# Two reorderings in a fused attention and Fourier-mixing kernel: the order of seven block products, and a transpose taken apart

## The chip, the core and the metric

The kernel runs on one core of a Trainium2 chip. The core has engines that each work through their own list of instructions in order and wait for one another through semaphores: PE (TensorE: matmuls and transposes; its weight loads are shown apart as PEld), DVE (VectorE), ACT (ScalarE), POOL (GpSimd) and SP (SyncE, which here only issues DMA transfers). The metric is the time of one execution on the device in microseconds (us), the median of several runs.

## The reference

Two stages, for 8 batches of 576 tokens, 8 heads of 64 channels (512 channels in all).

```
scores = q @ k.T / 8                            # per batch and head, 576 x 576
keep the 32 largest of each row (>= the 32nd), others -1e9
x = softmax(scores) @ v                         # heads put side by side: 576 x 512
u = x + real(fft(fft(x, axis=tokens), axis=channels))
un = (u - mean(u)) / sqrt(var(u) + 1e-6)        # over the channels
out = u + relu(un @ w_ch1) @ w_ch2              # w_ch1: 512 x 2048, w_ch2: 2048 x 512
```

## The kernel before, in words

**Attention.** The 32 pairs of heads (four to a batch; `PER_PAIR` = 9 work items to a pair, `PER_BATCH` = 36 to a batch, 288 in all) run through one main loop over steps `i` (L1589). An item is 128 rows of scores. In step `i` PE makes the scores of item `i + 3`, ACT evicts them (L396, L414, L425), DVE finds the 32nd largest value of item `i` and `i + 1` by alternating MAX8 and MATCH_REPLACE8 (L446, L448: seven long instructions to an item), and ACT and POOL mask and exponentiate items `i - 1` and `i - 2` (L469, L472, L480). From the second batch on the probabilities go by ACT copies and DMA (L493, L506, L509) to DRAM and come back transposed (L527); PE then multiplies them by v (`attend`, L585), and the result is turned to token rows (`to_tokens`, L626) and normalised by DVE (L630).

**q and k.** `prep` (L309) transposes the next pair's q or k on PE (L329) into a PSUM tile with the tag `tp`, which has two buffers, and ACT evicts it (L337, L339). For q it is called at every step with `i % 9 == 0` from the second batch on, with two blocks: four 128-token blocks (the main block) go to one `tp` buffer, and the tail block, made of `qtail`, to the next one. The partial scores `sp_t` (L392, evicted at L396) use the same two buffers.

**The mixing and the two-layer product.** When a batch's attention is done, the Fourier mixing (POOL folds at L685 to L762, PE at L809 to L864) and the normalisation follow, and the two matmuls of the MLP are cut into units that wait in a list, `queue`. A unit is one hidden tile (`hidden`, L1046) or a part of the second product (`back`, L1075; `fast`, L1155). The units carry a planned cost in us (1.75 for most, 2.13 or 1.71 for a hidden tile). After each entry of the step's list `fixed` the loop calls `some`, which puts out units as long as the planned room of the step lasts, and after an entry that stands in `preps` at least up to a limit of 1.1, which is one unit:

```
got += some(max(room * (n + 1) / len(fixed) - got, 1.1 if fn in preps else 0.0))
```

What a step puts out over its room is carried over (`carry`) and taken from the room of the next.

**Seven products.** For the first chunk of batches 1 to 7 (counted from 0) and the second chunk of batches 6 and 7, `fast` makes the second product of four 128-token by 4 blocks with seven block products instead of eight. There are nine such places. Each of p1 to p7 is put out in two halves (`part` 0 and 1), and each half is a unit. Two PSUM banks are held throughout, `cv` and `cw`: p2 writes the low half of `cv`, p5 the high half, p3 adds to the high half; p1 writes the low half of `cw`, p4 its high half (in the last batch a third bank, `cz`), p6 and p7 add to the low half. After its second half each product is read out of its bank by ACT (L1225), in the last batch by DVE (L1211). Left factors are made in place by `mix` (L1193, run at L1198 on POOL, in the last steps on DVE): "21" before p5, "11" and "12" after p1, "22" after p4. Combined parts of the second weight matrix lie in DRAM (`scr`, shown as `w_parts`) and are fetched by `bring` (L973, L976, issued on SP) over the part that was used last: T1 into `w2_12` at the begin (for p5), T4 into `second` after each half of p2 (for p4), T2 into `w2_12` after each half of p5 (for p6), T3 into `second` after each half of p4 (for p7), then the originals back.

Of the kernel before, what the change touches and what calls it, by code (L numbers as in the profile page):

```python
# [86 lines left out]
def kernel(  # L87
# [15 lines left out]
    NC = 5  # L103
    NF = NC - 1
# [4 lines left out]
    NPB = H // 2  # L109
# [199 lines left out]
    def prep(n, pair, blocks=((0, NF), (NF, NC))):  # L309

        if pair >= NPAIR:
            return 0.0
        src, got_of = nat[n, pair], qT_of if n == "q" else kT_of
        if pair not in got_of:
            got_of[pair] = attp.tile(
                [P, S if n == "q" else NF * P], F32, name=f"{n}T_{pair}", tag=f"{n}T",
                bufs=2 if n == "q" else 1
            )
        t_sb = got_of[pair]
        for c0, c1 in blocks:  # L320
            tp = ps_t.tile([P, 4, P], F32, name=f"tp{n}_{pair}_{c0}", tag="tp")
            for c in range(c0, c1):
                block, turn_by = src[:, c, :, :], ident
                if n == "q":
                    turn_by = turns[:, 2 if c == NF else c % 2, :]
                    if c == NF:
                        hp = pair % NPB
                        block = qtail[:, 2 * hp:2 * hp + 2, :]
                nc.tensor.transpose(  # L329
                    tp[:, c - c0, :], block.rearrange("p h d -> p (h d)"), turn_by  # L330
                )
            if c0 < NF:
                dst, got = t_sb[:, c0 * P:c1 * P], tp.rearrange("p a c -> p (a c)")[:, 0:(c1 - c0) * P]
            else:
                dst, got = t_sb[:, NF * P:], tp[:, 0, 0:TAIL]
            if n == "q":
                nc.scalar.mul(out=dst, in_=got, mul=scale)  # L337
            elif c0 < NF:
                nc.scalar.copy(out=dst, in_=got)  # L339
            else:  # L340
                for e in range(2):
                    r = slice(D * e, D * (e + 1))
                    nc.scalar.copy(out=kt_t[r, TAIL * e:TAIL * (e + 1)], in_=tp[r, 0, 0:TAIL])
        return 0.7
# [696 lines left out]
    def mlp_units(b):  # L1041
        x = x_of[b]
        last = b == B - 1
# [111 lines left out]
        def fast(ch):  # L1155
# [164 lines left out]
            def begin():  # L1320
# [6 lines left out]
                (0.0, lambda: mix("21", "21", "22", ALU.add), "back")  # L1327
            ] + [
                (1.75, lambda f=f, part=part: f(part), "back")
                for f in (p2, p5, p1, p4, p6, *((p7, p3) if last and ch else (p3, p7)))  # L1330
                for part in range(2)
            ]

# [1 line left out]
        for ch in range(2):  # L1335
            units += [
                (8 * CW[ch] / 1200.0, lambda ch=ch, it=it: hidden(ch, it), ("hidden", b, ch))
                for it in range(NIT)
            ]
            seven = b and ch == 0 or b >= B - 2  # L1340
            if seven:
                begin, products = fast(ch)
                if ch == 0:
                    begins.append(begin)
                else:
                    units.insert(1 - NIT, (0.0, begin, ("hidden", b, 1)))
                mix_first = products.pop(0)
                units.append(mix_first)
            for t in [t for t in CHUNKS[ch] if t == 4 or not seven]:
                units += [  # L1350
                    (1.75, lambda ch=ch, t=t, p=p: back(ch, t, p), "back")
                    for p in range(4 if t == 4 else 8)
                ]
            if seven:
                units += products
# [127 lines left out]
    for b in range(B):  # L1483
        end = PER_BATCH * (b + 1) - 1
        last = b == B - 1
# [54 lines left out]
    def chunk_at(i):  # L1540

        for tile in (i - 5, i - 4, i - 3, i - 2):
            r = tile % PER_PAIR
            if PER_BATCH <= tile < N and r in (4, 8):
                if i - tile == ((5 if r == 4 else 4) if by_dma(tile) else 2 if tile in (2 * PER_BATCH - 1, N - 1) else 3):
                    return tile // PER_PAIR, r // 8
        return None, None
# [41 lines left out]
    while i < N + 5 or plan or queue or sums:  # L1589
        now[0] = i  # L1590
        run(i, "begin")
        pair_of = i // PER_PAIR
# [10 lines left out]
        preps = []  # L1603

        q_step = i == 2 if pair_of == 0 else i % PER_PAIR == 0
        if i < N and q_step:
            preps.append(lambda: prep("q", pair_of + 1))
        if i < N and i % PER_PAIR == 5:
            preps.append(lambda: prep("k", pair_of + 1))
        last_scores = []  # L1610
# [75 lines left out]
        pair, ch = chunk_at(i)  # L1686
# [81 lines left out]
```

## Time and profile before

| what | value |
|---|---|
| median of 3 runs | 1776.76 us (1775.06 to 1779.67) |
| the profiled execution | 1780.27 us, span from its first to its last instruction 1778.5 us |
| PE busy | 1632.1 us, 92% |
| DVE busy | 1552.5 us, 87% |
| ACT busy | 1278.8 us, 72% |
| POOL busy | 906.6 us, 51% |
| DMA queue of SP | 243.80 MB, 52.5% of 16 engines' span |

The times of the trace are those of the one profiled execution. A row of the timeline reads: start in us, length in us, engine, line, operation, what it writes and reads, shapes, how many instructions the row joins, and in brackets how long the engine had been idle and what ended that. A product of `fast` shows as 16 matmuls of 128x256. Because matmuls are pipelined, the time from the start of one group to the start of the next says more than the length of a group. `q` after an engine's name (SPq) means its issuing side.

### The profile page before, as it was taken

What the parts mean: (1) busy time and instruction counts of PE and PEld (TensorE: products, weight loads), DVE (VectorE), ACT (ScalarE), POOL (GpSimd) and SP (SyncE); (2) the same over time, 40 slices, a digit from 0 to 9 for tenths busy, and PEclk for the clock granted to TensorE, in tenths of its full rate; (3) what the DMA queues carried; (4) which work ended last, traced back from release to release, by engine and by line L of the source; (5) the groups of instructions that cost most, each with busy time, mean ns of one, the idle gap of its engine ahead of it and who ended that gap; (6) DMA issues with size and microseconds to landing.
All of it is one profiled execution on the core that took longest, in us unless ns stands there. A gap on an engine that the chain in (4) does not pass through costs nothing.

```text
span 1778.5 us, 26295 instructions
## 1 busy us (share of the span) xinstructions
PE 1632.1 (92%) x7830; PEld 1040.9 (59%) x7830; DVE 1552.5 (87%) x3319; ACT 1278.8 (72%) x3136; POOL 906.6 (51%) x1268
## 2 busy tenths in 40 slices
PE   5666689999898989999999999999999999999998
PEld 3444455464455755566555755576566755577777
DVE  7999989999999999998999999999999999863121
ACT  6888759887787878876888778877978787653200
POOL 4768846655634565354544665356535564333000
PEclk7778799999999999999999999999999999999999
DMA  5333126651457855586557856595558655643151
GB/s 156 115 102 117 32 81 163 185 152 50 119 145 196 222 131 135 136 233 161 135 136 200 212 133 140 152 240 145 152 132 222 182 135 128 172 114 101 36 180 60
DMA packets 492926, 255.28 MB, mean 144 GB/s; under 512 B 364528, under 2 KB 483056, under 8 KB 492784
## 3 DMA queue, kind: packets, MB, share of 16 engines
q1 hardware_dynamic: 489008, 243.80, 52.5%
q0 software_dynamic: 2816, 9.44, 1.6%
q8 instruction: 63, 1.03, 0.2%
q14 instruction: 79, 0.65, 0.1%
q10 hardware_dynamic: 960, 0.36, 0.1%
HBM read 99.79 MB, written 84.74 MB: 104 GB/s over the span
## 4 chain that ended last, share of the span: by engine, by line
PE 48%; DVE 16%; ACT 16%; POOL 14%; issue 5%; DMA 2%; POOLq 0%; SPq 0%; DVEq 0%; ACTq 0%
PE hp L1055 18%; DVE m L446 7%; DVE wk L448 6%; PE o L585 6%; PE cw L1254 5%; POOL wk L472 5%; PE cv L1254 4%; PE sp L422 4%; ACT wk L469 3%; POOL fold L696 3%; PE cp L1120 2%; ACT wk L493 2%; PE cp L1082 2%; ACT S L425 2%; PE sp_t L392 1%
## 5 line engine op out<-in xcount | busy, mean ns | idle before, releaser
L472 POOL TENSOR_TENSOR wk<-S,wk 128x576 f32<-128x576 f32 x288 | 407.6, 1415 | 418.1 <-ACT wk L469 417.2
L446 DVE MAX8 m<-wk 128x8 f32<-128x576 f32 x864 | 617.4, 741 | 0.1
L1055 PE MATMUL hp<-unT,w 128*128 128x256 f32 (+1 forms) x2048 | 529.6, 409 | 6.8 <-ACT hT L1059 6.0
L1055 PEld LDWEIGHTS hp<-unT,w 128*128 128x128 f32 x2048 | 378.0, 191 | 112.0 <-ACT hT L1059 11.4
L448 DVE MATCH_REPLACE8 wk<-m,wk 128x576 f32<-128x576 f32 x576 | 424.8, 737 | 0.0
L469 ACT ACTIVATE wk<-S,nt 128x576 f32<-128x576 f32 x288 | 224.3, 779 | 96.8 <-POOL nt L455 96.3
L493 ACT COPY wk<-S 128x576 uint16<-128x576 uint16 x468 | 290.2, 673 | 0.0
L446 DVE MAX8 m<-S 128x8 f32<-128x576 f32 x288 | 214.5, 745 | 11.6 <-ACT S L396 11.6
L480 ACT ACTIVATE S<-wk,nt 128x576 f32<-128x576 f32 x234 | 185.1, 791 | 46.7 <-POOL wk L472 45.4
L448 DVE MATCH_REPLACE8 wk<-m,S 128x576 f32<-128x576 f32 x288 | 212.5, 738 | 0.0
L1082 PE MATMUL cp<-w,hT 128*128 128x512 f32 x448 | 206.0, 598 | 0.0
L1059 ACT ACTIVATE hT<-hp 128x320 f32<-128x320 f32 (+1 forms) x256 | 104.1, 411 | 140.7 <-PE hp L1055 139.7
L585 PE MATMUL o<-PT,v 128*64 128x256 f32 (+3 forms) x1440 | 196.1, 417 | 5.6 <-DVE wk L448 2.1
L422 PE MATMUL sp<-kT,qT 64*128 64x512 f32 (+1 forms) x528 | 160.1, 668 | 6.7 <-ACT S L414 3.6
L585 PEld LDWEIGHTS o<-PT,v 128*64 128x64 f32 x1440 | 113.2, 154 | 84.1 <-issue 24.8
L425 ACT COPY S<-sp 128x512 f32<-128x512 f32 (+1 forms) x264 | 141.7, 589 | 26.2 <-PE sp L422 25.2
L455 POOL TENSOR_TENSOR nt<-m,cc 128x2 f32<-128x2 f32 x288 | 58.7, 204 | 166.9 <-DVE m L446 160.4
L1254 PE MATMUL cw<-w,hT 128*128 128x256 f32 x512 | 119.7, 383 | 9.1 <-ACT ct L1225 6.2
L1082 PEld LDWEIGHTS cp<-w,hT 128*128 128x128 f32 x448 | 81.3, 193 | 75.1 <-issue 74.7
L392 PEld LDWEIGHTS sp_t<-kt,qT 128*128 128x128 f32 x320 | 51.7, 195 | 111.4 <-issue 73.3
L1254 PEld LDWEIGHTS cw<-w,hT 128*128 128x128 f32 x512 | 94.5, 190 | 27.3 <-ACT ct L1225 8.4
L1254 PE MATMUL cv<-w,hT 128*128 128x256 f32 x432 | 100.4, 383 | 6.6 <-DMA w<-w_parts 2.8
(155 smaller groups left out, 2036.3 us busy)
## 6 DMA issues: line engine op xcount, KB each, us to landing
planes<-wk SPq DMA_DIRECT2D x208, 288.0 KB, 2.7
w<-w_parts SPq DMA_DIRECT2D x94, 512.0 KB, 4.7
space<-in_moe_w_ch_dram SPq DMA_DIRECT2D x32, 512.0 KB, 3.6
nat<-in_q_dram SPq DMA_DIRECT2D x128, 64.0 KB, 2.3
v<-in_v_dram SPq DMA_DIRECT2D x32, 256.0 KB, 3.4
nat<-in_k_dram SPq DMA_DIRECT2D x62, 128.0 KB, 2.8
planes<-wk SPq DMA_DIRECT2D x52, 144.0 KB, 2.7
w_parts<-w_t POOLq DMA_DIRECT2D x8, 512.0 KB, 4.0
```

What stands on the lines that cost most here:

```text
L422: nc.tensor.matmul(sp[r], lhsT=qT[hd, q_cols], rhs=kT[hd, :], start=True, stop=True)
L425: nc.scalar.copy(out=s_t[r, keys], in_=sp[r])
L446: ops.append(lambda src=src, m8=m8: nc.vector.max(out=m8, in_=src))
L448: ops.append(lambda src=src, m8=m8: nc.vector.match_replace(w, m8, src, NEG))
L469: nc.scalar.activation(out=w, in_=Ssb[i], func=AF.Relu, scale=-FAR, bias=Nt[i][:, 1:2])
L472: nc.gpsimd.tensor_tensor(out=w, in0=Ssb[i], in1=w, op=ALU.subtract)
L480: nc.scalar.activation(out=Ssb[i] if by_dma(i) else w, in_=w, func=AF.Exp, bias=Nt.pop(i)[:, 0:1], accum_out=den_t[pair % 3][:, c:c + 1],)
L493: nc.scalar.copy(out=words[:, half, :], in_=src[:, half, :])
L585: nc.tensor.matmul(o[D * e:D * (e + 1), c0:c1], lhsT=vv[:, e, c, :], rhs=pt[:, NF if c == NF else (NF + 1) * e + c, c0:c1], start=(c == 0) ...
L1055: nc.tensor.matmul(hp[:, 0:w], lhsT=w1[:, dt, P * it:P * (it + 1)], rhs=unT[:, dt, 0:w], start=(dt == 0), stop=(dt == NDT - 1),)
L1082: nc.tensor.matmul(cp, lhsT=hT[:, it, P * n:P * (n + 1)], rhs=w2[:, it, :], start=(it == 0), stop=(it == NIT - 1),)
L1254: nc.tensor.matmul(dst, lhsT=h()[a][:, kc, :], rhs=rhs_of(kc), start=start and kc == 0, stop=kc == NK - 1, skip_group_check=True,)
```

## The change

Two edits. In `fast` the products p1 and p5 change places, so that the order is p2, p1, p5, p4, p6, p3, p7 (p7, p3 at the very last place). In the main loop, from the second batch on, q's preparation is entered into `preps` as two entries, the main block and the tail block, each with half the planned cost; through the rule above, a unit is put out after each of the two.

```
@@ -1327,7 +1327,7 @@
                 (0.0, lambda: mix("21", "21", "22", ALU.add), "back")
             ] + [
                 (1.75, lambda f=f, part=part: f(part), "back")
-                for f in (p2, p5, p1, p4, p6, *((p7, p3) if last and ch else (p3, p7)))
+                for f in (p2, p1, p5, p4, p6, *((p7, p3) if last and ch else (p3, p7)))
                 for part in range(2)
             ]
 
@@ -1604,7 +1604,11 @@
 
         q_step = i == 2 if pair_of == 0 else i % PER_PAIR == 0
         if i < N and q_step:
-            preps.append(lambda: prep("q", pair_of + 1))
+            if pair_of < NPB:
+                preps.append(lambda: prep("q", pair_of + 1))
+            else:
+                for blocks in ((0, NF),), ((NF, NC),):
+                    preps.append(lambda blocks=blocks: prep("q", pair_of + 1, blocks) / 2)
         if i < N and i % PER_PAIR == 5:
             preps.append(lambda: prep("k", pair_of + 1))
         last_scores = []
```

More of the change, by code (lines that the diff above doesn't have):

```diff
@@ L1329, in fast @@
                 (1.75, lambda f=f, part=part: f(part), "back")
-                for f in (p2, p5, p1, p4, p6, *((p7, p3) if last and ch else (p3, p7)))
+                for f in (p2, p1, p5, p4, p6, *((p7, p3) if last and ch else (p3, p7)))
                 for part in range(2)
@@ L1606 @@
         if i < N and q_step:
-            preps.append(lambda: prep("q", pair_of + 1))
+            if pair_of < NPB:
+                preps.append(lambda: prep("q", pair_of + 1))
+            else:
+                for blocks in ((0, NF),), ((NF, NC),):
+                    preps.append(lambda blocks=blocks: prep("q", pair_of + 1, blocks) / 2)
         if i < N and i % PER_PAIR == 5:
```

## The prediction

> **What bounds the kernel now.** I read the busy times, then a table by stages, then PE's timeline for every gap, then DVE's gaps, and last SP's queue around the seven products.
>
> ```profile
> PE 1632.1 (92%) x7830; PEld 1040.9 (59%) x7830; DVE 1552.5 (87%) x3319; ACT 1278.8 (72%) x3136; POOL 906.6 (51%) x1268
> 1150.00:1200.00 50.00, 48.06 (x239) 33.39 (x233) 46.83 (x100) 38.22 (x88) 27.51 (x33) 1.00 0.91 237
> 1400.00:1450.00 50.00, 49.47 (x239) 30.86 (x237) 48.17 (x103) 38.55 (x101) 30.53 (x52) 1.00 0.54 140
> 1700.00:1750.00 50.00, 49.74 (x230) 43.82 (x231) 8.34 (x15) 6.13 (x16) 0.98 (x2) 1.00 0.38 123
> ```
>
> The columns of the last three rows are busy us of PE, PEld, DVE, ACT and POOL, the granted clock, the DMA share and GB/s. From the third batch to about 1500 us PE and DVE are both nearly full; which of them sets the pace changes within each batch. At the end PE is alone, so there every gap of PE is time. In the middle a gap of PE is time only where DVE in turn waits for PE.
>
> All gaps of PE that stand between p2 and p5 (first eight rows; the second place of batch 6 has none) and between p1 and p4 (last seven):
>
> ```profile
> 562.16 3.69 PE L1254 MATMUL cv<-w,hT 128*128 128x256 f32 x16 [2.79 <-DMA w<-w_parts]
> 770.42 3.69 PE L1254 MATMUL cv<-w,hT 128*128 128x256 f32 x16 [0.61 <-issue]
> 968.19 3.69 PE L1254 MATMUL cv<-w,hT 128*128 128x256 f32 x16 [0.61 <-issue]
> 1161.58 3.69 PE L1254 MATMUL cv<-w,hT 128*128 128x256 f32 x16 [0.28 <-issue]
> 1355.04 3.69 PE L1254 MATMUL cv<-w,hT 128*128 128x256 f32 x16 [0.28 <-issue]
> 1541.40 3.69 PE L1254 MATMUL cv<-w,hT 128*128 128x256 f32 x16 [0.79 <-issue]
> 1700.26 3.72 PE L1254 MATMUL cv<-w,hT 128*128 128x256 f32 x16 [0.58 <-DVE x L1211]
> 1752.90 3.72 PE L1254 MATMUL cv<-w,hT 128*128 128x256 f32 x16 [0.58 <-DVE x L1211]
> 575.32 1.99 PE L1254 MATMUL cw<-w,hT 128*128 128x256 f32 x8 [1.61 <-ACT ct L1225]
> 781.92 1.99 PE L1254 MATMUL cw<-w,hT 128*128 128x256 f32 x8 [0.56 <-ACT ct L1225]
> 979.69 1.99 PE L1254 MATMUL cw<-w,hT 128*128 128x256 f32 x8 [0.56 <-ACT ct L1225]
> 1173.08 3.72 PE L1254 MATMUL cw<-w,hT 128*128 128x256 f32 x16 [0.56 <-ACT ct L1225]
> 1366.53 3.72 PE L1254 MATMUL cw<-w,hT 128*128 128x256 f32 x16 [0.56 <-ACT ct L1225]
> 1554.73 1.99 PE L1254 MATMUL cw<-w,hT 128*128 128x256 f32 x8 [2.33 <-ACT ct L1225]
> 1626.57 3.72 PE L1254 MATMUL cw<-w,hT 128*128 128x256 f32 x16 [0.56 <-ACT hT L1225]
> ```
>
> The reason shows in the releasers: p5 writes the other half of the bank that p2 has just filled, and waits until ACT or DVE has read p2 out; p4 waits for p1's reading in the same way.
>
> **The change part by part.** *The swap removes these waits.* In the order p2, p1, p5, p4 the bank changes every time, so each reading has a whole product of other work before its bank is written again. How long that is, and what a gap costs, the last batch shows:
>
> ```profile
> 1695.96 3.72 PE L1254 MATMUL cv<-w,hT 128*128 128x256 f32 x16
> 1703.81 3.62 PE L1254 MATMUL cw<-w,hT 128*128 128x256 f32 x16
> 1707.27 3.62 PE L1254 MATMUL cz<-w_s,hT 128*128 128x256 f32 x16
> 1710.72 3.62 PE L1254 MATMUL cw<-w,hT 128*128 128x256 f32 x16
> ```
>
> From cz to cw it is 1710.72 - 1707.27 = 3.45 us for a product; the longest wait for ACT above, 2.33, fits into it. From p2 to p5 it is 1700.26 - 1695.96 = 4.30, 0.85 for a gap of 0.58. So a gap costs itself and about 0.2. The first eight make 6.52, the other seven 6.74; with 0.2 each, 16.3 us of PE time. The swap adds no instruction. The waits p4 to p6 stay, since both write `cw` in either order. Mixes "11" and "12" are queued a product earlier, p5's T1 is needed a product later (that is the 2.79); neither costs anything.
>
> *What of it is time.* These are DVE's waits for PE behind the products, in batches 1 to 5:
>
> ```profile
> 580.88 0.42 DVE L630 TENSOR_TENSOR x<-tpx,rd 128x256 f32<-128x256 f32 x1 [1.31 <-PE tpx L626]
> 786.45 0.42 DVE L630 TENSOR_TENSOR x<-tpx,rd 128x256 f32<-128x256 f32 x1 [1.29 <-PE tpx L626]
> 984.22 0.42 DVE L630 TENSOR_TENSOR x<-tpx,rd 128x256 f32<-128x256 f32 x1 [1.29 <-PE tpx L626]
> 1179.63 0.42 DVE L630 TENSOR_TENSOR x<-tpx,rd 128x256 f32<-128x256 f32 x1 [3.14 <-PE tpx L626]
> 1564.60 0.42 DVE L630 TENSOR_TENSOR x<-tpx,rd 128x256 f32<-128x256 f32 x1 [6.07 <-PE tpx L626]
> ```
>
> Batch 1: PE saves 2.79 + 1.61 + 0.4 = 4.8, DVE can gain only its 1.31: 1.3. Batches 2 and 3: PE 0.61 + 0.56 + 0.4 = 1.57, DVE 1.29: 1.3 each, 2.6. Batches 4 and 5: PE 0.28 + 0.56 + 0.4 = 1.24, and DVE waits longer than that: 1.24 each. Batch 6, first place: 0.79 + 2.33 + 0.4 = 3.52, DVE waits 6.07, all of it counts; second place 0.56 + 0.2 = 0.76; batch 7: 2 x (0.58 + 0.25) = 1.66. From there on PE has no other gap to speak of, so these 5.9 are time.
>
> *What the swap makes late: T2.* Its two transfers go into `w2_12` after the halves of p5 and p6 reads them. So far p1 and p4 lie between, afterwards p4 alone: one product, 3.45, less lead.
>
> ```profile
> w<-w_parts SPq DMA_DIRECT2D x94, 512.0 KB, 4.7
> 1702.28 2.09 SPq L976 DMA_DIRECT2D w<-w_parts  x2
> 1163.45 1.16 SPq L976 DMA_DIRECT2D w<-w_parts  x2
> 1164.70 0.55 SPq L506 DMA_DIRECT2D planes<-wk  x1
> 1172.26 2.33 SPq L527 DMA_TRANSPOSE PT<-planes  x1
> 1175.35 0.56 SPq L976 DMA_DIRECT2D w<-w_parts  x1
> 1177.41 1.97 PE L1254 MATMUL cw<-w,hT 128*128 128x256 f32 x8
> ```
>
> In the last batch T2 goes out 1702.28 - 1700.26 = 2.0 after p5's start and lands 4.7 later, at 6.7; p6 is due two products after p5's start, at 6.9. It just fits, no cost. In batches 4 and 5, though, SP is not free: T2, now the second of the pair at 1163.45 and a single one behind 1164.70, moves one step on, behind the transpose L527, which starts at 1172.26 when the planes of 1164.70 have landed. With one 512 KB transfer less ahead of those planes (2.2 us at the 237 GB/s of the stage) L527 starts near 1170, ends near 1172.4, the planes write behind it takes 0.6, and T2 lands near 1173 + 4.7 = 1177.7. p6 starts at 1177.41 now and without the gaps near 1176.2; it would wait some 1.5. Bounds: no wait, if the landing is early; or T2 goes out only where T3 does now, 1175.35, and lands at 1180.05, 3.9 late. I take 1.2, which eats the saving: 0 for batches 4 and 5, between -2.5 and +5.4 for the two. In batches 2 and 3 no half of p4 shares a step with p5, so T2 has a step of its own, and I count nothing; at worst the wait eats their 2.6. In batch 6 p4 and p6 stand a step behind p5 as well.
>
> [...]
>
> *The q split.* PE waits for the tail's buffer. The group of all tails, one of the four gaps that are alike in batches 3 to 6, and what stands around it:
>
> ```profile
> L329 PE MATMUL tpq<-turns,qtail 128*128 128x128 f32 x32 | 9.9, 309 | 9.5 <-ACT S L396 9.2
> 1245.40 0.33 PE L329 MATMUL tpq<-turns,qtail 128*128 128x128 f32 x1 [0.54 <-ACT S L396]
> 1242.24 0.78 ACT L469 ACTIVATE wk<-S,nt 128x576 f32<-128x576 f32 x1 [2.27 <-POOL nt L455]
> 1256.18 0.77 ACT L1108 ACTIVATE hT<-cp,gi 128x512 f32<-128x512 f32 x1
> 1257.85 0.76 DVE L446 MAX8 m<-S 128x8 f32<-128x576 f32 x1 [1.59 <-ACT S L396]
> ```
>
> Before the 32 tails PE idled 9.5 us. A unit (some 1.75 by its planned cost) between main and tail fills most of that. But ACT, which PE waits for, itself waits for POOL's bounds and so for DVE's top values (2.27): PE is ahead of DVE there, and what it gains it will wait later. I count nothing. Since a unit is put out after each half, a q step carries one unit more, and the next step one less. What is queued behind it: the batch's dft, its ACT evictions and the scores for which DVE waits at 1257.85. PE reaches these up to 1.2 later (1.75 less 0.54), four times: +5 if ACT were waiting for PE there. But ACT comes to that score straight from L1108, which belongs to the unit that moves and goes with it into the q step: down to -0.77 four times, -3. Between these I take 0.
>
> Sum: 1.3 + 2.6 + 0 + 5.9 + 0 = 9.8 us less. On the profiled 1780.27 that is 1770.5; this execution was 3.5 above the median, so I take it from the median: 1776.76 - 9.8 = **1767.0**.
>
> **The rivals.** *DVE sets the pace up to 1600.* Its busy 48.17 of 50 speaks for it, its waits of 1.3 to 3.1 for PE against. Then only batch 6's second place and batch 7 count, 2.4: 1774. [...] The waits of DVE on PE behind the products are against it.
>
> *The q waits pay too.* If PE's lead lasts until the next place where DVE waits for it, the four small ones (0.54 + 0.2) and half of ACT's 3 come on top, 4.5 us: 1762.5. For it: DVE's wait at 1257.85. Against: it hangs on ACT, whose wait at 1242.24 is for DVE.
>
> *T2 is late everywhere, slower.* Place: p6 in batches 2 to 6. Price: T2 lands as in the upper bound, 1180.05, while p6 starts at 1177.41 now: 2.6 later than before, with the token transposes and so DVE's L630 behind it, five times 13; less batch 1's and the end's 1.3 + 2.4: +9.3, 1786. It decides from the point where T2 leaves SP less than 4.7 before p6 is due. For it: the DMA share 0.91 in this stage. Against: the lead of 6.9 in the last batch, and that in batches 2, 3 and 6 T2 has a step of its own.
>
> **How the numbers follow.** Forecast 0.60, late T2 0.13, DVE's pace 0.15, the q waits 0.12. 0.3% is 5.3 us, about what this kernel's measurement can tell from no change, so the line lies at 1771.4. The bounds of the forecast are -9.8 - 2.5 - 3 - 3.5 (the rest of batch 1), about -19, and -9.8 + 5.4 + 5 + 2.6, about +3: 1758 to 1780, not all at once, so its own range is 1760 to 1778. The whole range, 1759 to 1780, leaves out the worse half of late T2. Faster: 0.60 x 0.9 + 0.12 = 0.66; same: 0.06 + 0.15 = 0.21; slower 0.13.
>
> **What would show it.** Right: no gap before `cv` at p5 and before `cw` at p4; in the last two places seven products 0.8 us shorter each; the waits at 580.88, 786.45 and 984.22 gone; no gap at the qtail beyond 1.3. Wrong: a gap before p6 that a DMA of `w_parts` ended, of more than 2 us; DVE's waits for `tpx` as long as before; DVE's wait for S, now 1.59, above 2.5 once in each batch.

## The result, and the profile after

The changed kernel takes 1775.30 us in the median (1771.46 to 1779.90, 22 runs), the kernel before in the same sessions 1777.58 (1774.97 to 1781.54, 22 runs). The ratio is 0.9987, 95% interval 0.9981 to 0.9993: 2.3 us faster where 9.8 were forecast. The span of the profiled execution is 1775.5 us, 3.0 below that of before.

The places that the prediction named, first in the changed kernel's PE timeline, the last batch's first chunk (p2, p1, p5, p4, p6, and the next):

```profile
1694.32 3.72 PE L1254 MATMUL cv<-w,hT 128*128 128x256 f32 x16
1697.88 3.62 PE L1254 MATMUL cw<-w,hT 128*128 128x256 f32 x16
1701.34 3.62 PE L1254 MATMUL cv<-w,hT 128*128 128x256 f32 x16
1704.79 3.62 PE L1254 MATMUL cz<-w_s,hT 128*128 128x256 f32 x16
1708.24 3.94 PE L1254 MATMUL cw<-w,hT 128*128 128x256 f32 x16
1712.02 3.62 PE L1254 MATMUL cv<-w,hT 128*128 128x256 f32 x16
```

From p2 to p1 it is 3.56, from p1 to p5 3.46: the 4.30 between p2 and p5 is gone, and at none of the nine places is there a gap before p5 or p4. Only p6 takes 3.78 from start to start instead of 3.45, because T2 lands just late: its second transfer lands at 1710.09, and p6's second half, which reads it, starts at 1710.22.

The table by stages, with the columns as before:

```profile
1150.00:1200.00 50.00, 49.02 (x255) 35.02 (x251) 48.03 (x102) 38.90 (x90) 29.25 (x35) 1.00 0.89 232
1400.00:1450.00 50.00, 49.04 (x238) 31.01 (x236) 46.86 (x100) 37.55 (x91) 32.00 (x55) 1.00 0.51 131
1700.00:1750.00 50.00, 49.91 (x231) 43.63 (x231) 8.16 (x14) 6.14 (x16) 0.96 (x1) 1.00 0.35 116
```

In the first stage PE and DVE do more in the same 50 us, in the last PE does; in the middle one DVE fell from 48.17 to 46.86, although nothing was meant to change there but q's preparation. To see where that comes from, I put the start of DVE's first MAX8 of the same item in both traces side by side:

| item | before | after | after less before |
|---|---|---|---|
| 100 (batch 1's products begin) | 564.94 | 564.32 | -0.62 |
| 104 | 586.25 | 584.42 | -1.83 |
| 108 | 606.97 | 608.67 | +1.70 |
| 144 | 796.43 | 795.97 | -0.46 |
| 148 | 820.72 | 820.40 | -0.32 |
| 152 | 843.15 | 840.28 | -2.87 |
| 156 | 863.38 | 860.05 | -3.32 |
| 160 | 886.51 | 885.58 | -0.93 |
| 192 | 1058.13 | 1055.15 | -2.97 |
| 196 | 1080.50 | 1079.87 | -0.64 |
| 228 | 1251.27 | 1248.84 | -2.43 |
| 232 | 1274.00 | 1273.56 | -0.44 |
| 264 | 1444.91 | 1445.27 | +0.36 |
| 268 | 1467.32 | 1470.01 | +2.69 |
| 280 | 1539.90 | 1542.28 | +2.38 |
| 284 | 1569.96 | 1569.62 | -0.33 |
| end of the span | 1778.5 | 1775.5 | -3.0 |

Gains come and are given back. Four losses are alike: 2.39 (items 156 to 160), 2.33 (192 to 196), 1.99 (228 to 232) and 2.33 (264 to 268), 9.0 us together, each at the q step with `i % 36 == 9` (i = 153, 189, 225 and 261), the second of its batch's four. The recorded texts call it the first q step of a batch; the condition in the edits below, `pair_of % NPB == 1`, means this one. A fifth, 3.53, follows the products of batch 1 (104 to 108). DVE's timeline of the changed kernel shows what it waits for there:

```profile
598.02 0.42 DVE L630 TENSOR_TENSOR x<-tpx,rd 128x256 f32<-128x256 f32 x1 [3.44 <-PE tpx L626]
867.49 0.19 DVE L612 RECIPROCAL rd<-rd 128x6 f32<-128x6 f32 x1 [2.53 <-ACT rd L611]
1061.78 0.19 DVE L612 RECIPROCAL rd<-rd 128x6 f32<-128x6 f32 x1 [1.73 <-ACT rd L611]
1255.48 0.19 DVE L612 RECIPROCAL rd<-rd 128x6 f32<-128x6 f32 x1 [1.75 <-ACT rd L611]
1451.93 0.19 DVE L612 RECIPROCAL rd<-rd 128x6 f32<-128x6 f32 x1 [1.75 <-ACT rd L611]
```

None of the four waits for rd exists before. ACT is late, and ACT's timeline says why:

```profile
858.68 0.72 ACT L1108 ACTIVATE hT<-cp,gi 128x512 f32<-128x512 f32 x1
863.04 0.78 ACT L469 ACTIVATE wk<-S,nt 128x576 f32<-128x576 f32 x1 [3.64 <-POOL nt L455]
...
864.86 1.51 ACT L414 COPY S<-sp 64x256 f32<-64x256 f32 x4
...
867.25 0.21 ACT L611 ACTIVATE rd<-den 128x6 f32<-128x6 f32 x1
```

ACT stands still 3.64 us for POOL's bound `nt`, which it needs for the next mask, and everything behind it in its queue, rd among it (the softmax sums that DVE inverts for the normalisation), is late. POOL's timeline, first before, then after:

```profile
861.07 2.15 POOL L762 TENSOR_TENSOR near<-fold 128x513 f32<-128x513 f32 x2
863.17 0.20 POOL L455 TENSOR_TENSOR nt<-m,cc 128x2 f32<-128x2 f32 x1
864.25 1.42 POOL L472 TENSOR_TENSOR wk<-S,wk 128x576 f32<-128x576 f32 x1 [0.89 <-ACT wk L469]
869.88 1.27 POOL L1110 TENSOR_TENSOR x<-x,hT 128x512 f32<-128x512 f32 x1 [4.21 <-ACT hT L1108]
```

```profile
856.40 1.41 POOL L472 TENSOR_TENSOR wk<-S,wk 128x576 f32<-128x576 f32 x1 [1.13 <-ACT wk L469]
859.48 1.28 POOL L1110 TENSOR_TENSOR x<-x,hT 128x512 f32<-128x512 f32 x1 [1.67 <-ACT hT L1108]
860.72 2.14 POOL L762 TENSOR_TENSOR near<-fold 128x513 f32<-128x513 f32 x2
862.82 0.19 POOL L455 TENSOR_TENSOR nt<-m,cc 128x2 f32<-128x2 f32 x1
```

The unit that the split brings into the q step is the last part of a block of the second product. It ends not with ACT's L1108 but with POOL's addition L1110. That addition used to stand behind the fold L762, the bound and the mask; now it stands ahead of all three, waits 1.67 us for ACT and takes 1.28. Fold and bound come 2.95 us later than POOL could have them.

### The profile page after: what moved, and what is told of

The parts are those of the page before. It is cut to its first block, busy times and chain, and to the rows that moved or that the text cites. A ratio compares the mean times of both kernels' runs of the same rounds, so it can differ in the third digit from the quotient of the medians.

```text
span 1775.5 us, 26303 instructions
## 1 busy us (share of the span) xinstructions
PE 1633.7 (92%) x7830; PEld 1045.9 (59%) x7830; DVE 1553.4 (87%) x3319; ACT 1279.0 (72%) x3136; POOL 907.4 (51%) x1268
## 4 chain that ended last, share of the span: by engine, by line
PE 53%; DVE 15%; ACT 13%; POOL 11%; issue 4%; DMA 3%; SPq 1%; POOLq 0%; DVEq 0%; ACTq 0%
PE hp L1055 22%; PE o L585 7%; DVE m L446 7%; DVE wk L448 6%; PE sp L422 4%; PE cw L1254 4%; PE cv L1254 4%; POOL wk L472 4%; POOL fold L696 3%; PE cp L1120 3%; ACT wk L469 3%; PE cp L1082 2%; PE sp_t L392 2%; ACT wk L493 1%; DMA w<-w_parts 1%
## 5 line engine op out<-in xcount | busy, mean ns | idle before, releaser
L446 DVE MAX8 m<-S 128x8 f32<-128x576 f32 x288 | 215.1, 747 | 10.1 <-ACT S L396 10.1
L585 PE MATMUL o<-PT,v 128*64 128x256 f32 (+3 forms) x1440 | 198.0, 420 | 7.1 <-DMA PT<-planes 3.6
L422 PE MATMUL sp<-kT,qT 64*128 64x512 f32 (+1 forms) x528 | 164.9, 666 | 10.3 <-ACT S L414 7.2
L585 PEld LDWEIGHTS o<-PT,v 128*64 128x64 f32 x1440 | 116.4, 156 | 83.4 <-issue 22.6
```

What stands on the lines that cost most here:

```text
L422: nc.tensor.matmul(sp[r], lhsT=qT[hd, q_cols], rhs=kT[hd, :], start=True, stop=True)
L446: ops.append(lambda src=src, m8=m8: nc.vector.max(out=m8, in_=src))
L585: nc.tensor.matmul(o[D * e:D * (e + 1), c0:c1], lhsT=vv[:, e, c, :], rhs=pt[:, NF if c == NF else (NF + 1) * e + c, c0:c1], start=(c == 0) ...
```

## The experiments

The theory: the change of places does about what was forecast, and the split costs 2.2 us at each of those four steps through POOL's queue. The rivals: the swap itself loses through late T2, or DVE sets the pace up to 1600 us and no gain counts there. All ratios are against the kernel before on the same chip; 0.1% is 1.8 us.

**The parts alone.** The first keeps only the first hunk of the change, the second only the second:

> The change of places alone, q's preparation as before. Theory A (the split of q costs about 2.2 us at the first q step of each of batches 4 to 7, where DVE's wait for rd L611 is 2.53, 1.73, 1.75 and 1.75 us after the change and not there before; the swap gives about what was forecast): 8.8 us below the changed kernel's 1775.3, so 1766.5, and those four waits are gone. Theory B (the split is free as predicted; the swap itself loses, because T2 comes late to p6): like the changed kernel, 1775, the four waits still there or replaced. Theory C (up to 1600 us DVE sets the pace and no gain counts there): about 2.4 below the kernel before, 1775, with DVE's waits for tpx no shorter in sum.

> The split of q alone, p1 and p5 in their old places. Theory A: about 8.8 us slower than the kernel before, 1786, with a new wait of DVE for rd L611 at the first q step of batches 4 to 7. Theories B and C: like the kernel before, 1777.6, within 1.5.

Measured: the change of places alone 0.9943 (0.9927 to 0.9959), 10.1 us faster; the split alone 1.0054 (1.0040 to 1.0069), 9.6 us slower. The four waits for rd are absent in the first and there in the second. So what the change gains and what it gives back are its two halves, each near 10 us.

**Which q steps.** The split stays out of, or is kept to, the second q step of each batch from the second batch on (e4 with the old order of the products):

```
e3:  -            if pair_of < NPB:
     +            if pair_of < NPB or pair_of % NPB == 1:
e4:  -            if pair_of < NPB:
     +            if pair_of < NPB or pair_of % NPB != 1:
```

> Both edits, but at the first q step of each batch the main block and the tail block stay one entry, so that no unit is added there; the other three q steps of a batch are split as in the change. Theory A in its narrow form (the loss sits only where the added unit's POOL addition L1110 goes into POOL's queue ahead of the mixing's fold L762): the whole 8.8 us come back, 1766.5, as with the swap alone. A wider form (each of the split q steps costs something): between 1766.5 and 1775. Theory B: 1775.

> The old order of the products, and the split only at the first q step of each batch from the third on. Theory A in its narrow form: as slow as the split everywhere, about 8.8 us above the kernel before, 1786. Theories B and C: like the kernel before, 1777.6.

Measured: 0.9941 (0.9924 to 0.9959) and 1.0052 (1.0038 to 1.0066). The second q steps carry the whole net loss; the split of the other three is worth nothing net.

**POOL's queue, or the unit itself.** Two edits to the whole change. The first (e5) runs the step's fold ahead of the list of PE work, so that L762 stands ahead of L1110; the second (e6) puts L1110 one step later:

```
e5:  +        early = i > 4 * PER_BATCH and i % PER_BATCH == PER_PAIR and i < N
     ...
     +        if early:
     +            run(i, "pool0")
     ...
     -        run(i, "pool0")
     +        if not early:
     +            run(i, "pool0")

e6:  -                        nc.gpsimd.tensor_tensor(out=xt, in0=xt, in1=ct, op=ALU.add)
     +                        def add():
     +                            nc.gpsimd.tensor_tensor(out=xt, in0=xt, in1=ct, op=ALU.add)
     +                        if now[0] > 4 * PER_BATCH and now[0] % PER_BATCH == PER_PAIR:
     +                            at(now[0] + 1, "begin", add)
     +                        else:
     +                            add()
```

> The whole change, but in the first q step of batches 4 to 7 POOL gets the fold L762 ahead of the added unit's addition L1110 (and behind both the bound nt, as in the change). Theory P (POOL's queue: the fold and nt stand behind an addition that first waits 1.67 us for ACT and takes 1.28): the fold runs during that wait; nt still stands behind the addition, so only about 1.5 of each 2.2 us comes back: 6 in all, 1769. Theory Q (the unit itself on PE or ACT, put ahead of the scores and the dft, costs the time): 1775, the four waits of DVE for rd as long as after the change, 1.7 to 2.5.

> The whole change, but in the same four steps the addition L1110 goes into POOL's queue one step later, behind the fold and nt; PE, ACT and DVE keep their orders. Theory P: all of the loss comes back, 8.8 us below the changed kernel's 1775.3, 1766.5, and DVE's four waits for rd are gone. Theory Q: 1775.

Measured: 0.9941 (0.9928 to 0.9953) with the fold first, 0.9921 (0.9898 to 0.9945) with the addition later. POOL's timeline with the fold first, and then with the addition later (the line numbers are shifted there):

```profile
859.04 2.14 POOL L762 TENSOR_TENSOR near<-fold 128x513 f32<-128x513 f32 x2
861.14 1.28 POOL L1110 TENSOR_TENSOR x<-x,hT 128x512 f32<-128x512 f32 x1
862.37 0.20 POOL L455 TENSOR_TENSOR nt<-m,cc 128x2 f32<-128x2 f32 x1
```

```profile
855.23 2.14 POOL L762 TENSOR_TENSOR near<-fold 128x513 f32<-128x513 f32 x2
857.33 0.19 POOL L455 TENSOR_TENSOR nt<-m,cc 128x2 f32<-128x2 f32 x1
857.47 1.29 POOL L1111 TENSOR_TENSOR x<-x,hT 128x512 f32<-128x512 f32 x1
858.71 1.42 POOL L472 TENSOR_TENSOR wk<-S,wk 128x576 f32<-128x576 f32 x1
```

The addition no longer waits in either; with the fold first the bound still has the 1.28 ahead of it, with the addition later nothing. DVE's wait for rd, 2.53 after the change, goes to 0.81 and then away:

```profile
867.05 0.19 DVE L612 RECIPROCAL rd<-rd 128x6 f32<-128x6 f32 x1 [0.81 <-ACT rd L611]
```

Between items 156 and 160 the changed kernel loses 2.39 us, the one with the fold first 0.65, and the one with the addition later gains 0.58. From the change to e6 the order of instructions is the same on PE, DVE, ACT and SP; on POOL four additions stand elsewhere. So the unit itself costs nothing there; it is POOL's order. The two steps, 1.74 and 1.23, are the addition's wait of 1.67 and its length of 1.28. Over all four places e5 gains 6.9 us on the changed kernel in the traces, and 8.2 by the ratios (6 expected); e6 gains 11.9, 2.95 to 2.97 at each, and 11.7 by the ratios (8.8 expected). That is more than the 9.0 lost against the kernel before, because with the addition out of the way these places are 0.6 to 1.0 us faster than before.

**Where the change of places pays.** Only in batches 6 and 7 (`b >= B - 2`), and only in batches 1 to 5:

```
     -                for f in (p2, p5, p1, p4, p6, *((p7, p3) if last and ch else (p3, p7)))
e7:  +                for f in (p2, *((p1, p5) if b >= B - 2 else (p5, p1)), p4, p6,
e8:  +                for f in (p2, *((p1, p5) if b < B - 2 else (p5, p1)), p4, p6,
```

> The change of places in batches 6 and 7 alone, no split. Theory F (as forecast, gains count where DVE in turn waits for PE): 3.5 + 0.8 + 1.7 = 5.9 below the kernel before, 1771.7. Theory C (DVE sets the pace up to 1600): 2.4 below, 1775.

> The change of places in batches 1 to 5 alone, no split. Theory F: 3.9 below the kernel before, 1773.7 (1.3 in each of the first three, 0 in the other two). Theory C: like the kernel before, 1777.6. From the waits before p6 for T2 that the swap alone showed in batches 3 and 5 (2.24 and 2.04 us, where the forecast had 0 and 1.2), somewhat less than theory F: 2 to 3 below.

Measured: 0.9957 (0.9944 to 0.9970), 7.7 us faster, in the late batches; 0.9996 (0.9985 to 1.0007), no difference, in the early ones. The late batches give what was forecast or a little more. The early ones look like the rival of DVE's pace, but the trace does not: DVE's waits at the products of batches 1 to 3 are gone there, 1.2 us each between the items. PE's timeline of this kernel shows what takes it back in batches 3, 4 and 5, p6 waiting for T2:

```profile
979.61 1.75 PE L1254 MATMUL cw<-w,hT 128*128 128x256 f32 x7 [1.42 <-DMA w<-w_parts]
1173.22 1.97 PE L1254 MATMUL cw<-w,hT 128*128 128x256 f32 x8 [2.08 <-DMA w<-w_parts]
1369.04 1.97 PE L1254 MATMUL cw<-w,hT 128*128 128x256 f32 x8 [3.09 <-DMA w<-w_parts]
```

At 657.58, in batch 3, this one execution also met a half-clock stretch that the kernel before does not have there (granted clock 0.54 from 657.60 to 661.30, before 1.00); it falls back 2.0 us between items 120 and 132, and the last section comes back to it. The next run takes T2 away from the same kernel:

```
e11: -                bring(T2, w2_12, part)
     +                if b >= B - 2:
     +                    bring(T2, w2_12, part)
```

> The change of places in batches 1 to 5 alone, as in the run that gave 0.9996, but T2 is not fetched in these batches, so that p6 multiplies by what is left in its place. Theory T (late T2 ate the gain: p6's waits for it of 1.42, 2.08 and 3.09 us in batches 3, 4 and 5): those waits are gone and 4 to 6 us below the kernel before come out, ratio 0.997 to 0.9965. Theory C (DVE sets the pace there): ratio 0.9996 as before, although the waits are gone.

Measured: 0.9955 (0.9942 to 0.9968), 8.0 us faster than before, more than the 4 to 6 expected, where the same order with T2 gave nothing. So T2's transfers, and not DVE's pace, eat the gain of the early batches. PE no longer waits for any transfer of `w_parts` before p6, and between items 212 and 216 (batch 4) the kernel gains 1.30 where it lost 0.82 with T2, between 248 and 252 (batch 5) it gains 1.30 where it lost 1.92. The run also moves five times 1 MB less, so it does not separate the waiting for T2 from the room that its transfers take; in batch 1, where p6 does not wait for T2, it still saves 0.85.

**What the split is worth with POOL's queue mended.** The split as in e6 with the old order of the products (e9), with the change of places in batches 6 and 7 only (e10), and the whole change with the addition later in one more step (e12: `now[0] >= 3 * PER_BATCH and now[0] % PER_BATCH in (PER_PAIR - 1, PER_PAIR)`):

> The split with the addition L1110 one step later in POOL's queue, and the old order of the products. Theory G (once POOL's queue is mended, the added unit fills waits of PE that count, as the difference between the whole change so mended and the swap alone suggests, 0.9921 against 0.9943): about 4 us below the kernel before, ratio 0.998. Theory H (the split is worth nothing by itself, as predicted): ratio 1.000 within 0.001.

> The split with the addition one step later, and the change of places in batches 6 and 7 alone. If the change of places in batches 1 to 5 is worth nothing (0.9996 alone): as fast as with all nine places changed, ratio 0.992. If it is worth the forecast 3.9 us there: 0.994 to 0.995.

> The whole change with the addition L1110 one step later, now also in the step before batch 3's first q step, where it stands ahead of the fold L696 in every kernel and waits 2.25 us for ACT. If POOL's order sets the pace there too: PE's wait of 1.77 us for the fold L762 near 664 and DVE's of 1.3 to 1.7 for S near 672 go, and the time is 1 to 2 us below that of the same kernel without it (ratio 0.9921), 0.991. If something else does: 0.992 and those waits stay.

Measured: 0.9991 (0.9983 to 1.0000), 0.9969 (0.9957 to 0.9981) and 0.9914 (0.9899 to 0.9929).

The first: mended, the split is worth next to nothing, 1.6 us. Against e2, which differs in the four additions alone, that is 1.0054 to 0.9991, 11 us for four times 2.95.

The second was a miss: with the mended split, the change of places in batches 1 to 5 is worth 0.9969 to 0.9921, 8.5 us, where it was worth 0.7 without the split. PE's timeline of e10 at batch 2's products shows the reason, p2's second half and then p5, and ACT's beside it:

```profile
768.71 1.89 PE L1259 MATMUL cv<-w,hT 128*128 128x256 f32 x8
772.62 5.38 PE L1259 MATMUL cv<-w,hT 128*128 128x256 f32 x16 [2.02 <-issue]
```

```profile
770.09 1.07 ACT L425 COPY S<-sp 128x512 f32<-128x512 f32 x2
...
772.02 0.49 ACT L1230 ACTIVATE ct<-cv,gi 128x256 f32<-128x256 f32 x1
```

With the split the units stand one further on. PE names no releaser for the 2.02, but p5 starts 0.11 after ACT has read p2 out (L1230 here, behind the evictions of scores): in the old order it waits 2.02 for that instead of the 0.61 before. Worse, the product then takes 5.38 instead of 3.69. e2, with a gap of 2.01 and a product of 5.38 at the same place, shows a granted clock of 0.68 there (772.70 to 778.10). DVE loses 2.99 there between items 140 and 144; with the places changed (e6) it gains 1.19. At the products of batches 1, 2 and 3 together e10 falls behind e6 by 2.85, 4.18 and 2.50, 9.5 us in the traces, about the 8.5 of the ratios. So in the old order the split has a cost that the change of places takes away. Whether the split in turn takes away what late T2 costs is not shown: in e6 p6 still waits up to 1.50 for it.

The third does not settle what it was made for. PE has no gap before the fold's readers near 667 any more, where e6 has 1.77, but not because the fold is earlier: L762 starts 1.93 us before DVE's first MAX8 of item 120 (666.14 and 668.07), in e6 2.40 before it (663.37 and 665.77). It is PE that comes later: its attend L585 starts 3.93 before that MAX8 (664.14), in e6 6.53 (659.24). DVE's wait for S stays, 1.73 after 1.29, and the time is that of e6 within the intervals. Whether POOL's order costs anything in that step stays open.

The version that beats both kernels is thus the whole change with the addition L1110 put out one step later: 1764.9 us in the median of its runs (e6), 0.9921 of before.

## Why the prediction was wrong

**The removed gaps: right.** All fifteen are gone, and p5's and p4's releasers with them. One thing that was to cost nothing, the mixes "11" and "12", did hold p6 up once: in batch 5 it waits 1.34 for POOL's L1198 (at 1369.82). In the last place the seven products take 0.85 less (1768.12 - 1746.56 = 21.56 from p2 to the last product's start after, 1771.12 - 1748.71 = 22.41 before); in the one ahead of it only 0.52, for p6's 0.33. In batches 1, 2 and 3 DVE's waits at 580.88, 786.45 and 984.22 went, and 1.2 came out at each.

**The tail: right.** 5.9 were counted for batches 6 and 7; 7.7 were measured alone, interval 5.3 to 10.0. In that run's trace batch 6's first place gives 3.63 (forecast 3.52) and the rest 2.98 (2.42).

**Late T2: right in kind, too small.** The step "I take 1.2, which eats the saving: 0 for batches 4 and 5" was a late landing of 1.2 (the working above it had come to 1.5). With the change of places in batches 1 to 5 alone (e8) the waits were 2.08 and 3.09, and these batches lost 0.8 and 1.9 instead of nothing; in the changed kernel itself they are 0.22 and 1.14, and batch 4 gains 1.2 and batch 5 loses 1.2. And "In batches 2 and 3 no half of p4 shares a step with p5, so T2 has a step of its own, and I count nothing" fell: after the change p6 waits there too, in PE's timeline:

```profile
786.92 3.26 PE L1254 MATMUL cw<-w,hT 128*128 128x256 f32 x14 [1.55 <-DMA w<-w_parts]
982.03 3.26 PE L1254 MATMUL cw<-w,hT 128*128 128x256 f32 x14 [1.47 <-DMA w<-w_parts]
```

In these two the gain of 1.2 came out all the same. For the early batches 3.9 were forecast and 0.7 measured alone (e8, interval -2.7 to +1.2 against before); without T2 (e11) it was 8.0. The bound that I gave for T2, up to 3.9 late, holds the waits.

**The q split: this step failed.** "But ACT comes to that score straight from L1108, which belongs to the unit that moves and goes with it into the q step: down to -0.77 four times, -3. Between these I take 0." I followed the moved unit on PE and on ACT and stopped there. Its last instruction is on POOL: L1110, 1.28 long, and on POOL it went from behind the fold and the bound to ahead of them, with its wait for ACT. That is 2.95 of delay, four times. Against the kernel before 2.0 to 2.4 of it show at DVE, 9.0 in the trace, and the split alone measured 9.6 slower; what the four additions alone are worth is 11 to 12 us (e2 against e9, the change against e6). The term taken as 0 was thus about +9, and the upper bound of +5 was also too low. The row that would have shown it was there before: POOL's L1110 at 869.88 with 4.21 of waiting for ACT's L1108, directly behind the mask. The tail's gaps did shrink as said (none is above 1.23 after the change), and it was worth next to nothing net, also as said. That 1775.3 still lies in the stated 1760 to 1778 is luck: the loss on POOL was not among the terms that made this range.

The sum of the measured parts, -10.1 and +9.6, is -0.5; the change itself is -2.3. Within the intervals (about 3 us for the parts) that is the same, so the interplay of the two edits that e10 shows is not resolved here.

**The rivals.** "DVE sets the pace up to 1600" came out near the right time, 1774, by luck and for the wrong reason: e11 and e6 gain in the middle. "The q waits pay too" is refuted by e9. "T2 is late everywhere" had its place right, batches 2 to 5, but its 13 us were too much, and p6's waits did not make the whole slower.

**What stays open.** In batch 1 every kernel that splits the q step within the products loses 3.3 to 5.4 us behind them (items 104 to 108), with the old order as with the new one, and no kernel without that split loses more than 1.1 between these items. After p6, which waits for p4's reading, PE waits there for transposed probabilities:

```profile
578.18 3.69 PE L1254 MATMUL cw<-w,hT 128*128 128x256 f32 x16 [2.40 <-ACT ct L1225]
585.11 3.73 PE L585 MATMUL o<-PT,v 128*64 128x256 f32 x20 [3.23 <-DMA PT<-planes]
```

Part of the loss is the clock, granted at 0.50 there and at 1.00 in the same 3.40 us of the kernel before. The attend behind the wait takes 3.73 us, where before it took 2.38; the row from the kernel before, and the window of the changed kernel:

```profile
584.75 2.38 PE L585 MATMUL o<-PT,v 128*64 128x256 f32 x20
584.50:587.90 3.40, 2.79 (x14) 1.89 (x16) 3.40 (x8) 1.48 (x3) 1.42 (x1) 0.50 0.92 227
```

PE's rows of other kernels with the split show matmuls as slow thereabouts: the attend takes 3.78 in e6 (at 582.89), p6 5.38 in e2, e9 and e10 (at 580.79, 580.57 and 581.29). In e8 and e11, which do not have the split, p6 takes 3.71 and 3.69 there and the attend 2.38. In the changed kernel the wait itself, 3.23, is the larger part. The transpose L527 that it waits for starts at 580.52, before at 578.05; two transfers of `w_parts` that SP put out at 564.16 before now go out at 571.28, behind an earlier transpose. Whether these are the reason for the wait was not tried.

## What to carry to other kernels

When a unit of work is moved, follow it to its last instruction on every engine, and look on each of those queues at what it is now ahead of; POOL, 51% busy here, still held DVE up by 2.0 to 2.4 us four times, because its queue is in order and the moved addition brought its wait of 1.67 us along. When a wait is removed on one engine, ask which transfer was hidden behind it. And test the halves of a change apart: a change near zero was here two of 10 us each, and a version that keeps both and moves one addition is 14 us faster than before.

## What the runs showed of the hardware that was not expected

A gap of PE of 2.01 us cost nearly twice what it is. The table of windows around the p5 of e2, which stands behind that gap (2.02 in e10), and around PE's gap of 2.10 at 825.69 in the kernel before (columns as above; the granted clock is the number behind the five busy times):

```profile
766.00:770.40 4.40, 4.40 (x25) 3.46 (x21) 4.37 (x10) 4.30 (x10) 1.27 (x1) 1.00 1.05 252
772.70:778.10 5.40, 5.36 (x18) 4.15 (x19) 5.40 (x13) 2.78 (x5) 2.28 (x3) 0.68 0.68 202
778.10:782.00 3.90, 3.90 (x29) 2.16 (x29) 3.90 (x9) 2.86 (x6) 3.12 (x4) 1.00 1.00 334
```

```profile
820.00:825.00 5.00, 3.60 (x18) 2.83 (x16) 4.82 (x12) 4.17 (x11) 2.94 (x4) 1.00 0.81 221
825.70:829.10 3.40, 3.40 (x20) 2.09 (x20) 3.40 (x8) 0.00 (x0) 0.00 (x0) 0.65 0.37 90
829.10:833.00 3.90, 3.90 (x19) 2.55 (x18) 1.42 (x4) 3.52 (x10) 2.35 (x4) 0.86 0.67 140
```

Behind e2's gap the granted clock is 0.68 over the 5.40 us of the product, which takes 5.38 instead of 3.69. Behind the gap in the kernel before it is 0.50 from 826.74 to 830.15, and the attend takes 3.55, where the one at 584.75 takes 2.38. So 2.01 us of gap cost 3.7 in all, and 2.10 cost 3.3. Not every gap does it. The same two instructions in the kernel before and in e8:

```profile
657.73 0.33 PE L329 MATMUL tpq<-turns,qtail 128*128 128x128 f32 x1 [2.96 <-ACT S L396]
657.89 1.88 PE L1082 MATMUL cp<-w,hT 128*128 128x512 f32 x4
```

```profile
657.58 0.45 PE L329 MATMUL tpq<-turns,qtail 128*128 128x128 f32 x1 [2.26 <-ACT S L396]
657.83 3.49 PE L1082 MATMUL cp<-w,hT 128*128 128x512 f32 x4
```

The longer gap left the four matmuls behind it at 1.88 us (granted clock 1.00), behind the shorter one they took 3.49 (0.54). In the changed kernel, from 300 us on, slow stretches begin at 379.7, 424.0, 451.3, 485.5 and 584.5. Each is 3.41 us long at a granted clock of 0.50, and they begin 44.4, 27.3, 34.1 and 99.0 us after one another, 13, 8, 10 and 29 times that length. In the 3.41 us ahead of each PE was idle for 2.1 to 2.8 us in sum. The kernel before has five as well, each 3.41 us long at 0.50, with 1.9 to 3.2 us of idle PE in the 3.4 us ahead. But it also has the gaps of 2.79 and 2.96 that end at 562.16 and 657.73, and behind both the granted clock is 1.00. What decides between them is not shown: no run was made to test it.

That also warns of reading one trace: the slow stretch behind 825.69 is in the kernel before and not in the changed one (granted clock 1.00 from 816 to 833). All later traces are 2.2 to 2.6 us faster between items 148 and 152, e4 and e7 too, in which nothing near there was changed for the better. Of the 3.0 us between the two profiled spans, 2.5 thus belong to this one place, while the changed kernel's trace has a slow stretch of its own at 584.5 that the kernel before lacks (granted clock 0.50 and 1.00). Spans of single traces don't carry a result of this size; the medians do.
